# Up products of the last batch as seven products of quarters

## The chip, the cores and the metric

The kernel runs on one core of one Trainium2 chip. The metric is the device time of one execution in microseconds (us). TensorE (PE in the profile) multiplies matrices and writes into PSUM, its accumulators, which come in banks of 512 fp32 columns; VectorE (DVE), ScalarE (ACT) and GpSimd (POOL) work on elements; SyncE (SP) issues most of the DMAs. A matmul on TensorE takes a weight tile of 128x128, loaded ahead by an instruction of its own (PEld), and streams a number of columns past it. Each engine takes its instructions in the order in which the kernel's code emits them.

## What is computed

Windowed attention with a few global keys (4 batches, 8 heads, 768 positions, head dimension 64), and then a mixer on its output x (4 x 768 x 512):

```python
h = xt @ U @ V                       # xt = x.transpose(0, 2, 1); rank 32
u = x + h.transpose(0, 2, 1)
ch = np.maximum(u @ w_ch1, 0.0) @ w_ch2      # 512 -> 2048 -> 512
return (u + ch).astype(np.float32)
```

The product `u @ w_ch1` is called *up* here, the product with `w_ch2` *down*.

## The kernel before

**Attention** runs over 16 pairs of heads, `i = 0..15`, four per batch, in one loop whose body is a list of steps written out by hand: scores (`st_S`), the exponential on ScalarE (`st_E`), the product with v (`st_V`), the low-rank part (`st_M1`, `st_MT`, `st_M3`), and a DMA transpose (`st_X`, L522) that writes one 128-row slice of `uT`, the transposed u in fp16. The instructions keep the order in which the code emits them (`manual_schedule`).

**The mixer** of batch b starts when its four slices of `uT` are on their way. `queue_ff(b)` calls `queue_group` for each of three groups of 256 tokens and puts closures into two queues, `ups_q` and `downs_q`. A call `fill(n)` between the steps of attention takes n units; `unit` takes ups and downs in turn, keeps a down product back until all ups of its group are out, and lets the ups run at most one group ahead. After the loop, `while ups_q or downs_q: fill(1)` empties both. After each unit `fill` also takes one job (two when more than four are waiting) out of `jobs`, or out of `slow` when `jobs` has none that is due; these are sums that VectorE makes. `need(...)` emits a sum that is still queued when its reader comes. Each sum goes through `queue_sum` (its instruction is at L571).

**An up unit** (`mk_up`) is eight matmuls of 256 columns (L653) into one bank, with the tag `th` (three banks): two 128-wide slices of hidden columns by four slices of 128 of the 512 inputs. A ReLU on ScalarE (L658) moves the bank's 512 columns to `htr` in fp16. Eight units make a group.

**The down side** of batches 1 to 3 is already made of seven products of quarters (`mk_product`, matmuls at L707, x1, y1, x2, y2, x3, y3, x4 in this order), each eight matmuls of 256 columns. Two banks (`cx`, `cy`, tag `cps`) collect them, and after each product VectorE adds the bank to `x_sb` (L712). Their left factors are quarters of `htr` (two halves of the hidden columns by two halves of the tokens) and the sums `s1` to `s4` of these; their right ones are quarters of `w_ch2` and the sums `t1` to `t4`, made once. `queue_sums` queues `s1` to `s4` for each half of the hidden columns' slices as the ReLUs come out.

**Buffers that the change touches.** `sp` (fp32 scores, one buffer) is last read by the exponential of pair 15; `ep` (exponentials, two buffers) by `st_V` of pairs 14 and 15; `qst`, `kst` and `vst` are the staging of q, k and v. In PSUM, `sc` (two banks) and `ob` (one) belong to attention.

Of the kernel before, what the change touches and what calls it, by code (L numbers as in the profile page):

```python
# [11 lines left out]
FP32 = mybir.dt.float32  # L12
FP16 = mybir.dt.float16
# [7 lines left out]
def kernel(  # L21
# [13 lines left out]
    nc = tc.nc  # L35
# [30 lines left out]
    HJ = NJC // 2  # L66
    HD = DM // 2
    WG = tuple((b, g) for b in range(1, B) for g in range(NFG))

    cst = ctx.enter_context(tc.tile_pool(name="cst", bufs=1))  # L70
    wbig = ctx.enter_context(tc.tile_pool(name="wbig", bufs=1))
# [8 lines left out]
    def ps_sc():  # L80

        return psum.tile([P, 2, 512], FP32, name="sc", tag="sc", bufs=1)

    def ps_ob():
        return psum.tile([P, 512], FP32, name="ob", tag="ob", bufs=1)
# [4 lines left out]
    def ps_th(name, dtype=FP32, cols=512):  # L90
        return psum.tile([P, cols], dtype, name=name, tag="th", bufs=3)
# [428 lines left out]
    def st_X(i):  # L520
        b, dc = i // NP, i % NP
        nc.sync.dma_start_transpose(  # L522
            uTs[b][:, dc].rearrange("d (n p) -> d n p", n=NSB),
            x16s[i].rearrange("p n d -> p (n d)"),
        )
# [42 lines left out]
    def queue_sum(name, part, out_, a, b_, op, wait=0):  # L568

        def go():  # L570
            nc.vector.tensor_tensor(out_, a, b_, op)  # L571
            have.add((name, part))
        (slow if name[0] == "t" else jobs).append((count[0] + wait, go, name))

    def need(*names):

        for queue, kind in ((jobs, tuple), (slow, str)):
            while not all(n in have for n in names if isinstance(n[0], kind)):
                queue.popleft()[1]()
# [19 lines left out]
    def weight(w, j):  # L599
        return tw[w][:, j] if w != "t3" else tw[w][j // 2][:, j % 2]  # L600

    first_ups = []

    def queue_ff(b):
        for g in range(NFG):
            queue_group(b, g)
        if b == 0:
            for c in range(4):
                for made in first_ups:
                    ups_q.extend(made[2 * c:2 * c + 2])  # L610

    def queue_group(b, g):
# [60 lines left out]
        def mk_down(t, part):  # L673
            n = 2 * g + t

            def go():
                if (b, g, t, part) == (0, 0, 1, 0):
                    queue_weight_sums()
                if part == 0:
                    cell[t] = ps_cps("cps")  # L680
                    if b == 0:
                        nc.tensor.matmul(
                            cell[t], v16w[:, n * P:(n + 1) * P], tmp16,
                            start=True, stop=False,
                        )
                cps, htr = cell[t], cell["htr"]
                for jc in range(4 * part, 4 * part + 4):
                    nc.tensor.matmul(  # L688
                        cps, htr[:, jc, t * P:(t + 1) * P], w2_16[:, jc],
                        start=(b > 0 and jc == 0), stop=(jc == NJC - 1),  # L690
                    )
                if part == NJC // 4 - 1:
                    nc.vector.tensor_tensor(x_sb[:, n], cps, x_sb[:, n], ALU.add)
                    store(n)
            return go
# [18 lines left out]
                    store(*what)  # L714
            return go

        if b:
            for at in range(NJC // 2):
                ups_q.append((mk_up(at), (b, g)))
        else:  # L720
            first_ups.append([(mk_up(at), (b, g)) for at in range(NJC // 2)])
        if split:
            x1 = mk_product("cx", lo, "a11", "b11", (n0, lo), first=True)
            x2 = mk_product("cx", lo, "s2", "t2", (n0, hi_))
            x3 = mk_product("cx", lo, "s3", "t3", (n1, hi_), done=[(n1, hi_)] if last else None)
            x4 = mk_product("cx", lo, "a22", "t4", (n1, lo), done=[(n1, lo)] if last else [(n1,)])
            y1 = mk_product("cy", lo, "a12", "b21", (n0, lo), first=True)
            y2 = mk_product("cy", hi_, "s1", "t1", (n1, hi_))
            y3 = mk_product("cy", hi_, "s4", "b22", (n0, hi_), done=[(n0,)])
            for made in (x1, y1, x2, y2, x3, y3, x4):  # L730
                downs_q.append((made, (b, g)))
        else:
            order = [(t, part) for t in range(2) for part in range(NJC // 4)]
            if (b, g) == (0, 0):
                order.sort(key=lambda u: max(1, u[1]))
            for u in order:
                downs_q.append((mk_down(*u), (b, g)))

    ahead, held, kept = [0], [True], deque()

# [2 lines left out]
    def fill(n, quiet=False):  # L743
        for _ in range(n):
            unit()
            count[0] += 1
            pops = owed[0] + (2 if len(jobs) > 4 else 1)
            owed[0] = 1 if quiet else 0
            if jobs and jobs[0][2][0] == "s1" and not (ups_q or drained[0]):
                pops = 2  # L750
            for _ in range(0 if quiet else pops):
                for queue in (jobs, slow):
                    if queue and queue[0][0] < count[0]:
                        queue.popleft()[1]()
                        break
# [79 lines left out]
    for i in range(NP, NPAIR + 2):  # L835
        b, hp = divmod(i, NP)
        live = i < NPAIR
        units = iter(
            (0, 1, 1, 2, 1, 1, 1, 1, 1) if i == NP
            else (0, 1, 1, 1, 1, 1, 1, 1, 1) if i + 1 < NPE  # L840
            else (1, 1, 1, 2, 1, 1, 1, 1, 1)
        )
        held[0] = i < NP + 3
        if hp == 0 and live and b + 1 < B:
            new_batch(b + 1)
        if live and i > NP:
            st_S(i, 0)
        if NPE <= i + 1 < NPAIR:
            turn(i + 1)
        if i + 1 < NPAIR and i != NP + 2:  # L850
            load_v(i + 1)
        if i + 2 < NPE:
            load_qk(i + 2)
        fill(next(units))
        if NPE + 2 <= i + 2 < NPAIR:
            cast_one(i + 2, 1, nc.scalar)
        if NP < i <= NPAIR:
            st_V(i - 1, 0)
        if i == NP:
            load_w1(2)  # L860
        if i + 1 < NPE:
            st_T(i + 1)
        if i == NP:
            load_w1(3)
        fill(next(units))
        joined = live and i >= NPE - 1
        if joined:
            mid = st_S12(i)
        elif live:
            st_S(i, 1)  # L870
        fill(next(units), quiet=i > NP + 1 and (i - 2) % NP == NP - 1)
        if NP < i <= NPAIR:
            st_V(i - 1, 1)
        if joined:
            s_dve(i, mid)
        if live:
            cast_v(i)
            st_A(i)
        if NPE + 2 <= i + 2 < NPAIR:
            cast_one(i + 2, 0, nc.scalar)  # L880
        if NPE <= i + 3 < NPAIR and i != NP + 2:
            load_qk(i + 3)
        if i > NP + 1 and (i - 2) % NP == NP - 1:
            queue_ff((i - 2) // NP)
            ahead[0] = 1
        if i == NPAIR + 1:
            break
        fill(next(units))
        if live and not joined:
            st_S(i, 2)  # L890
        fill(next(units))
        if i > NP:
            st_M1(i - 1)
        else:
            for xo, o, rb in later:
                nc.vector.tensor_tensor(xo, o, rb, ALU.mult)
        if i == NP + 1:
            load_w2(0)
            load_w2(1)
        if i + 2 < NPE:  # L900
            cast_qk(i + 2, nc.gpsimd)
        if i == NP + 1:
            load_w2(2)
            load_w2(3)
        if live:
            st_E(i, 0)
            if i < NPE:
                st_P(i)
        fill(next(units), quiet=i > NP)
        if i > NPE:  # L910
            for _ in range(min(2, len(kept))):
                kept.popleft()()
        if i > NP:
            st_MT(i - 1)
        if NPE <= i + 1 < NPAIR:
            st_K(i + 1)
        fill(next(units))
        if i > NP:
            st_M3(i - 1)
        if live:  # L920
            st_E(i, 1)
        if i > NP + 1:
            st_X(i - 1)
        fill(next(units))
        if i == NP + 1:
            load_v(i + 2)
            load_qk(i + 4)
            st_X(i - 1)
        if i == NPE:
            for _ in range(2):  # L930
                kept.popleft()()
        if NPE <= i + 2 < NPE + 2:
            cast_qk(i + 2, nc.gpsimd)
        held[0] = i < NP + 2
        fill(next(units))
# [39 lines left out]
```

## Time and profile before

| | |
|---|---|
| median of 3 runs (lowest to highest) | 228.5 us (228.26 to 228.91) |
| the profiled execution: its own time, its span | 227.39 us, 225.6 us |
| busy share of the span: PE, PEld | 97%, 76% |
| busy share of the span: DVE, ACT, POOL | 69%, 56%, 33% |
| granted TensorE clock | 1.00 |
| up matmuls of 256 columns (L653), all batches | 756, 273 ns each |
| up ReLUs (L658) | 96, 600 ns each |

The span runs from the first instruction of the program to the last; the time of the execution is 1.8 us longer. Durations are those of single instructions; matmuls overlap, so the time from one start to the next is shorter than the duration. The text calls engines by name; lines of the profile use the short forms. "L653" is line 653 of the kernel before. In the rows of groups the columns are line, engine, operation, output<-inputs, shapes and count, then busy time and the mean of one in ns, then idle time before them and what ended it.

### The profile page before, as it was taken

To read this page: it belongs to the slowest core of one execution; us is meant where nothing else is said; L and a number is where in the kernel's file an instruction comes from. 1 tells how busy PE (TensorE), PEld (TensorE's weight loads), DVE (VectorE), ACT (ScalarE), POOL (GpSimd) and SP (SyncE) were. 2 spreads that over 40 slices of the span, in tenths; PEclk is the share of its full clock that TensorE was granted. 3 is DMA by queue.
4 is the path that set the end of the run, shared out by engine and by line. 5 is a ranking of instruction groups with operands and counts; after the bars stand their busy time and mean duration, and the time that the engine had idled before them with its cause. 6 is when DMAs were issued, how large, how long until landed. Compare 5 with 4: busy or idle time off the path is not lost.

```text
span 225.6 us, 5876 instructions
## 1 busy us (share of the span) xinstructions
PE 218.0 (97%) x2420; PEld 171.4 (76%) x2420; DVE 156.1 (69%) x320; ACT 126.2 (56%) x197; POOL 73.8 (33%) x124
## 2 busy tenths in 40 slices
PE   7989999999999999999999999999999999999993
PEld 2456678788754547888888888888998888888882
DVE  3798665749488988598989698898575534435552
ACT  6777867685806254967584947473733433333320
POOL 6498828297547412231313132313111000000000
PEclk9999999999999999999999999999999999999999
DMA  6999999969998999998989994960622102020112
GB/s 193 316 287 257 283 219 238 324 120 172 195 169 177 195 230 232 209 255 200 195 224 220 252 229 116 140 170 12 102 59 77 53 1 96 0 93 3 46 49 94
DMA packets 86563, 36.68 MB, mean 163 GB/s; under 512 B 74152, under 2 KB 83592, under 8 KB 86536
## 3 DMA queue, kind: packets, MB, share of 16 engines
q1 hardware_dynamic: 81480, 32.01, 60.6%
q0 software_dynamic: 5056, 4.29, 12.7%
q8 instruction: 19, 0.31, 0.6%
q14 instruction: 8, 0.07, 0.1%
HBM read 27.46 MB, written 6.29 MB: 150 GB/s over the span
## 4 chain that ended last, share of the span: by engine, by line
PE 85%; DVE 8%; ACT 2%; DMA 2%; issue 0%; SPq 0%
PE hps L653 35%; PE cx L707 13%; PE cy L707 10%; PE cps L688 9%; PE sc L367 3%; PE tp L254 3%; PE ob L448 2%; PE ob L444 2%; PE sc L533 2%; DMA kst<-in_k_dram 2%; PE sc L374 2%; ACT ep L431 1%; DVE x_sb L467 1%; DVE sp L413 1%; DVE x_sb L712 1%; DVE kA L290 1%
## 5 line engine op out<-in xcount | busy, mean ns | idle before, releaser
L653 PE MATMUL hps<-uT,w 128*128 128x256 f16 x756 | 95.0, 273 | 0.0
L658 ACT ACTIVATE htr<-hps 128x512 f16<-128x512 f32 x96 | 56.6, 600 | 55.7 <-PE hps L653 55.7
L653 PEld LDWEIGHTS <-w 128*128 128x128 f16 x756 | 71.2, 98 | 9.1
L413 DVE SCALAR_TENSOR_TENSOR sp<-sc,relcat 128x1024 f32<-128x1024 f32 (+1 forms) x27 | 32.1, 1189 | 8.5 <-PE sc L374 4.1
L431 ACT ACTIVATE ep<-sp 128x1408 f16<-128x1408 f32 x24 | 33.2, 1384 | 0.0
L470 POOL CAST x<-x_sb 128x384 f16<-128x384 f32 x27 | 14.2, 527 | 48.3 <-DVE x_sb L467 44.8
L707 PEld LDWEIGHTS <-htr 128*128 128x128 f16 x288 | 27.2, 98 | 3.1
L712 DVE TENSOR_TENSOR x_sb<-cx,x_sb 128x256 f32<-128x256 f32 x36 | 15.2, 421 | 19.0 <-PE cx L707 18.3
L688 PE MATMUL cps<-w,htr 128*128 128x512 f16 x96 | 23.9, 379 | 0.0
L707 PEld LDWEIGHTS <-s 128*128 128x128 f16 x216 | 20.4, 98 | 2.7
L541 POOL CAST x<-x_sb 128x768 f16<-128x768 f32 x12 | 10.2, 851 | 31.2 <-DVE x_sb L538 31.2
L712 DVE TENSOR_TENSOR x_sb<-cy,x_sb 128x256 f32<-128x256 f32 x27 | 11.4, 422 | 12.6 <-PE cy L707 12.4
L467 DVE TENSOR_TENSOR x_sb<-ob,rcp 128x384 f32<-128x384 f32 x30 | 16.7, 558 | 1.1
L367 PEld LDWEIGHTS <-kT 64*128 64x128 f16 x192 | 8.6, 93 | 11.5 <-issue 10.1
L448 PE MATMUL ob<-v,ep 128*128 128x65 f16 x192 | 16.4, 194 | 0.0
L367 PE MATMUL sc<-qT,kT 64*128 64x128 f16 x192 | 15.7, 220 | 0.0
L448 PEld LDWEIGHTS <-ep 128*128 128x128 f16 x192 | 13.8, 98 | 2.0 <-issue 0.3
L688 PEld LDWEIGHTS <-htr 128*128 128x128 f16 x96 | 8.4, 98 | 8.3
L444 PE MATMUL ob<-vA,ep 128*128 128x65 f16 x160 | 14.3, 194 | 0.2 <-DVE vA L317 0.2
L142 POOL CAST v<-vst 128x768 f16<-128x768 f32 x16 | 13.5, 842 | 3.0 <-DMA vst<-in_v_dram 3.0
L538 DVE TENSOR_TENSOR x_sb<-sc,x_sb 128x768 f32<-128x768 f32 x12 | 11.5, 958 | 4.0 <-PE sc L533 3.9
L374 PE MATMUL sc<-qT,kA 64*128 64x128 f16 x160 | 13.3, 217 | 0.8 <-DVE kA L290 0.6
(111 smaller groups left out, 319.2 us busy)
## 6 DMA issues: line engine op xcount, KB each, us to landing
qst<-in_q_dram SPq DMA_DIRECT2D x16, 384.0 KB, 4.0
kst<-in_k_dram SPq DMA_DIRECT2D x16, 384.0 KB, 5.7
vst<-in_v_dram SPq DMA_DIRECT2D x16, 384.0 KB, 4.0
out_dram<-x_sb SPq DMA_DIRECT2D x23, 256.0 KB, 2.0
w<-in_moe_w_ch_dram POOLq DMA_DIRECT2D x8, 512.0 KB, 8.1
vA<-v SPq DMA_DIRECT2D x8, 152.3 KB, 3.3
out_dram<-x_sb SPq DMA_DIRECT2D x2, 128.0 KB
uT<-x SPq DMA_TRANSPOSE x12, 4.4
```

The costliest lines, as they stand in the source:

```text
L367: nc.tensor.matmul(scs[hi][:, o:o + P], kT[r, kb * P:(kb + 1) * P], qT[r, kb * P:(kb + 1) * P], start=(o == 0 and not on_pe), stop=(o + P ...
L374: nc.tensor.matmul(scs[hi][:, o + P:o + 2 * P], kA[r, kb], qT[r, (kb + 1) * P:(kb + 2) * P], start=False, stop=(o + 2 * P == tot),)
L413: nc.vector.scalar_tensor_tensor(out=sps[i][:, :, c0:c0 + tot], in0=both[:, :, 0:tot], scalar=qk_scale / slope[2 * (i % NP)], in1=relfs[c0 ...
L431: nc.scalar.activation(eps[i][:, hi], sps[i][:, hi], AF.Exp, scale=slope[2 * (i % NP)])
L444: nc.tensor.matmul(ob[:, qi], ep[:, OF[qi - 1]:OF[qi - 1] + P], vA[:, qi - 1, hi], start=True, stop=False,)
L448: nc.tensor.matmul(ob[:, qi], ep[:, DG[qi]:DG[qi] + P], vt[:, qi, hi], start=(qi == 0), stop=True,)
L467: nc.vector.tensor_tensor(xo, ob[:, :, 0:D], rb, ALU.mult)
L653: nc.tensor.matmul(hps[:, k * FT:(k + 1) * FT], w1_16[:, dc, jt * P:(jt + 1) * P], uT[:, dc, ts], start=(dc == 0 and k == 0), stop=(dc == ...
L658: nc.scalar.activation(cell["htr"][:, 2 * jp:2 * jp + 2].rearrange("p j t -> p (j t)"), hps, AF.Relu)
L688: nc.tensor.matmul(cps, htr[:, jc, t * P:(t + 1) * P], w2_16[:, jc], start=(b > 0 and jc == 0), stop=(jc == NJC - 1),)
L707: nc.tensor.matmul(ps, cell[a][:, j], weight(w, j), start=(first and j == 0), stop=(done is not None and j == HJ - 1), skip_group_check=True,)
L712: nc.vector.tensor_tensor(x_sb[:, n, cs], ps, x_sb[:, n, cs], ALU.add)
```

## The change

For the last batch (`WU`), the up product of a group is written as u's transpose in quarters: A is `w_ch1` transposed in quarters (two halves of hidden columns, two halves of inputs), B is `uT` in quarters (two halves of inputs, two halves of the 256 tokens). Seven products take the place of eight. The hidden columns are handled in two parts `st` of 8 slices each (4 from each half), so a group has 14 products instead of 8 up units. A product is eight matmuls of 128 columns: four slices of hidden columns by two of inputs.

- **Weight sums**, `s1` to `s4` of quarters of `w_ch1`, for both parts: eight sums of 128x1024 fp16 on VectorE. Those of part 0 go into staging buffers (`qst`, `kst`), those of part 1 into the room that `sp` had. `queue_up_sums` puts the first four into `slow` at the end of step i = 15 and three more at the end of step i = 16; the eighth is emitted after row 4.
- **Token sums**, `t1` to `t4` of quarters of `uT`: four of 128x256 per group on VectorE, into rooms that `ep` had, emitted after the rows that `between` names.
- **Products.** In each part, products 1, 6, 7 and 4 accumulate in one bank of `th` (x), product 2 goes to the bank of `ob` (z), products 5 and 3 accumulate in one of the two banks of `sc` (y). After 2, 3 and 5 ScalarE copies the bank to SBUF (`p2`, `p3`, `p5`). After 1, 6 and 7 VectorE adds the x bank and one of these copies into a quarter of `htr`, and ScalarE applies the ReLU there in place. After 4 ScalarE applies the ReLU from the bank.
- **Rows.** The units in `ups_q` are now 22 rows (8, 7 and 7 per group), most with two products, in an order written out by hand:

```diff
+        for _, g in WU:
+            first = g == WU[0][1]
+            if first:
+                rows += [[(g, 0, 2), (g, 0, 1)], [(g, 0, 5), (g, 0, 6)], [(g, 0, 3), (g, 1, 5)]]
+            else:
+                rows[-2].insert(0, (g, 0, 5))
+                rows[-1].insert(0, (g, 0, 2))
+                rows += [[(g, 0, 1), (g, 0, 3)], [(g, 0, 6), (g, 1, 5)]]
+            rows += [[(g, 1, 2), (g, 0, 7)], [(g, 1, 1), (g, 0, 4)], [(g, 1, 3), (g, 1, 6)],
+                     [(g, 1, 7)], [(g, 1, 4)]]
+        between = {k: uw["sums"][1][x:x + 1] for k, x in ((4, 3),)}
+        for k, (_, g) in enumerate(WU):
+            for at, x in ((7 * k - 2, (0, 1)), (7 * k, (2,)), (7 * k + 1, (3,))):
+                if k == 0:
+                    at += 2
+                between.setdefault(at, []).extend(todo[g][y] for y in x)
```

The triples are group, part, product. The product itself:

```diff
+            bank, a, t = {
+                1: ("x", "a11", "b11"), 2: ("z", "a12", "b21"), 3: ("y", "s4", "b22"),
+                4: ("x", "a22", "t4"), 5: ("y", "s1", "t1"), 6: ("x", "s2", "t2"),
+                7: ("x", "s3", "t3"),
+            }[k]
...
+            for j in range(4):
+                for dc in range(2):
+                    nc.tensor.matmul(
+                        ps[:, j * P:(j + 1) * P], uw[st][a][:, dc, j * P:(j + 1) * P],
+                        turns[g][t][:, dc], start=(k in (1, 2, 5) and j == 0 and dc == 0),
+                        stop=(k in (2, 3, 4) and j == 3 and dc == 1), skip_group_check=True,
+                    )
+            early = g == WU[0][1] and st == 0
+            if k in (2, 3, 5):
...
+                nc.scalar.copy(part["p5", st] if k == 5 else part[f"p{k}"], ps)
+            if k == 1:
+                add(g, st, 0, 0, ps, part["p2"])
+            elif k == (3 if early else 6):
+                add(g, st, 0, 1, made[at, "x"], part["p3"])
+            elif k == 7:
+                add(g, st, 1, 1, ps, part["p5", st])
+            elif k == 4:
+                nc.scalar.activation(
+                    out_of(g, st, 1, 0), ps.rearrange("p (j t) -> p j t", j=4), AF.Relu
+                )
+                sums[g](st)
```

`add` is one VectorE add and one in-place ReLU:

```diff
+            nc.vector.tensor_tensor(to, x, y, ALU.add)
+            nc.scalar.activation(to, to, AF.Relu)
```

The groups of the last batch no longer put `mk_up` into `ups_q`; the down products and their sums are as before.

More of the change, by code (lines that the diff above doesn't have):

```diff
@@ L68 @@
     WG = tuple((b, g) for b in range(1, B) for g in range(NFG))
+    WU = tuple((B - 1, g) for g in range(NFG))
     cst = ctx.enter_context(tc.tile_pool(name="cst", bufs=1))
@@ L600, in weight, with up_sums @@
         return tw[w][:, j] if w != "t3" else tw[w][j // 2][:, j % 2]
+    uw, part = {}, {}
+    def up_sums():
+        made = {0: [], 1: []}
+        room = scp.tile([P, 2 * W], FP32, name="uw", tag="sp", bufs=1)
+        later_set = room[:, 0:16 * P].bitcast(FP16).rearrange("p (x d n) -> p x d n", x=4, d=2)
+        part["p2"] = room[:, 16 * P:20 * P]
+        for st in range(2):
+            js = [slice(h * DFF // 2 + st * 4 * P, h * DFF // 2 + (st + 1) * 4 * P) for h in range(2)]
+            w = {f"a{h + 1}{d + 1}": w1_16[:, 2 * d:2 * d + 2, js[h]] for h in range(2) for d in range(2)}
+            for x in range(4):
+                if st == 0:
+                    tag = ("qst", "kst")[x % 2]
+                    w[f"s{x + 1}"] = stp.tile([P, 2, 4 * P], FP16, name="uw", tag=tag, bufs=2)
+                else:
+                    w[f"s{x + 1}"] = later_set[:, x]
+            uw[st] = w
+            for name, a, b_, op in (
+                ("s1", "a21", "a22", ALU.add), ("s2", "s1", "a11", ALU.subtract),
+                ("s4", "a12", "s2", ALU.subtract), ("s3", "a11", "a21", ALU.subtract),
+            ):
+                made[st].append((f"tw{name}", st, w[name], w[a], w[b_], op))
+        return made
@@ new lines, in queue_up_sums, with token_sums @@
+    def queue_up_sums(st):
+        if st == 0:
+            uw["sums"] = up_sums()
+        for k, x in enumerate(uw["sums"][st][0:3 if st else 4]):
+            queue_sum(*x, wait=k)
+    turns = {}
+    def token_sums(g, t):
+        uT = uTs[B - 1]
+        q_ = {f"b{d + 1}{h + 1}": uT[:, 2 * d:2 * d + 2, g * FT + h * P:g * FT + (h + 1) * P]
+              for d in range(2) for h in range(2)}
+        q_.update({f"t{x + 1}": t[:, x] for x in range(4)})
+        turns[g] = q_
+        return [(f"tu{g}{n}", 0, q_[n], q_[a], q_[b_], ALU.subtract) for n, a, b_ in (
+            ("t1", "b12", "b11"), ("t2", "b22", "t1"), ("t3", "b22", "b12"), ("t4", "b21", "t2")
+        )]
@@ new lines, in queue_products, with out_of, add, step @@
+    def queue_products(b, cells, sums):
+        yy = ps_sc()
+        made = {}
+        rooms = [scp.tile([P, W], FP32, name="tu", tag="ep") for _ in range(2)]
+        places = [rooms[g // 2][:, g % 2 * 4 * P:(g % 2 + 1) * 4 * P] for g in range(NFG)]
+        part["p3"] = rooms[1][:, 4 * P:8 * P]
+        todo = {
+            g: token_sums(g, places[g].bitcast(FP16).rearrange("p (x d n) -> p x d n", x=4, d=2))
+            for _, g in WU
+        }
+        def out_of(g, st, h, t):
+            return cells[g]["htr"][:, h * HJ + 4 * st:h * HJ + 4 * st + 4, t * P:(t + 1) * P]
+        def add(g, st, h, t, x, y):
+            to = out_of(g, st, h, t)
+            x, y = (z.rearrange("p (j t) -> p j t", j=4) for z in (x, y))
+            nc.vector.tensor_tensor(to, x, y, ALU.add)
+            nc.scalar.activation(to, to, AF.Relu)
+        def step(g, st, k):
+            at = (g, st)
+            if "htr" not in cells[g]:
+                cells[g]["htr"] = ffp.tile([P, NJC, FT], FP16, name="htr", tag="htr", bufs=3)
+            if k == 1:
+                made[at, "x"] = ps_th("hps")
+            elif k == 2:
+                made[at, "z"] = ps_ob()
+            elif k == 5:
+                made[at, "y"] = yy[:, st]
+            bank, a, t = {
[3 more added lines that the diff above has]
+            }[k]
+            if a[0] == "s":
+                need((f"tw{a}", st))
+            if t[0] == "t":
+                need((f"tu{g}{t}", 0))
+            ps = made[at, bank]
+            for j in range(4):
[7 more added lines that the diff above has]
+            if k in (2, 3, 5):
+                if k == 5:
+                    part["p5", st] = stp.tile([P, 4 * P], FP32, name="p5", tag="vst", bufs=2)
+                nc.scalar.copy(part["p5", st] if k == 5 else part[f"p{k}"], ps)
+            if k == 1:
+                add(g, st, 0, 0, ps, part["p2"])
[8 more added lines that the diff above has]
+                sums[g](st)
+        rows = []
+        for _, g in WU:
+            first = g == WU[0][1]
+            if first:
+                rows += [[(g, 0, 2), (g, 0, 1)], [(g, 0, 5), (g, 0, 6)], [(g, 0, 3), (g, 1, 5)]]
+            else:
+                rows[-2].insert(0, (g, 0, 5))
[9 more added lines that the diff above has]
+                between.setdefault(at, []).extend(todo[g][y] for y in x)
+        def mk_row(n):
+            def go():
+                for s_ in rows[n]:
+                    step(*s_)
+                for x in between.pop(n, ()):
+                    nc.vector.tensor_tensor(*x[2:])
+                    have.add(x[:2])
+            return go
+        for n, row in enumerate(rows):
+            ups_q.append((mk_row(n), (b, row[-1][0])))
@@ L602 @@
     first_ups = []
     def queue_ff(b):
+        cells, sums = {}, {}
         for g in range(NFG):
-            queue_group(b, g)
+            cells[g], sums[g] = queue_group(b, g)
+        if (b, 0) in WU:
+            queue_products(b, cells, sums)
         if b == 0:
@@ L715, in mk_product @@
             return go
-        if b:
+        if (b, g) in WU:
+            pass
+        elif b:
             for at in range(NJC // 2):
@@ L737, in queue_group @@
                 downs_q.append((mk_down(*u), (b, g)))
+        return cell, queue_sums
     ahead, held, kept = [0], [True], deque()
@@ L923 @@
             st_X(i - 1)
+        if NPAIR - 1 <= i:
+            queue_up_sums(i - NPAIR + 1)
         fill(next(units))
```

## The prediction

> **What bounds the kernel now.** I read the page first, then the chain of waits over the last 50 us, then the windows of that stretch, then its groups of instructions by shape.
>
> ```profile
> PE 218.0 (97%) x2420; PEld 171.4 (76%) x2420; DVE 156.1 (69%) x320; ACT 126.2 (56%) x197; POOL 73.8 (33%) x124
> ...
> PE   7989999999999999999999999999999999999993
> ...
> DVE  3798665749488988598989698898575534435552
> ```
>
> TensorE (PE) is busy 97% of the span, VectorE (DVE) is nearly full while attention lasts and half idle in the last quarter. The chain of waits, start and duration first, shows who sets the pace there:
>
> ```profile
> 176.38 0.87 PE cx L707 x8
> 177.25 0.87 PE hps L653 x8
> 178.13 0.87 PE cy L707 x8
> ...
> 187.74 1.75 PE hps L653 x16
> ```
>
> Blocks of eight matmuls follow each other with no gap: 0.873 us for eight of 256 columns, 109.2 ns each. Up blocks (hps, L653) alternate with down products (cx, cy). By the timeline the last batch's 24 up blocks run from 177.1 to 215.5; after them come seven down products, and the last add and its store. So this stretch is bound by TensorE alone. The windows (PE, PEld, DVE, ACT, POOL, then clock, DMA share, GB/s) and the groups show what room its helpers have:
>
> ```profile
> 177.10:215.50 38.40, 38.40 (x354) 34.42 (x352) 17.45 (x41) 13.77 (x23) 0.00 (x0) 1.00 0.10 37
> ```
>
> ```profile
> L653 PE MATMUL hps<-uT,w 128*128 128x256 f16 x192 | 24.4, 273 | 0.0
> ...
> L712 DVE TENSOR_TENSOR x_sb<-cx,x_sb 128x256 f32<-128x256 f32 x12 | 5.1, 424 | 12.6 <-PE cx L707 12.4
> ```
>
> VectorE is busy 17.45 of 38.4 us, ScalarE (ACT) 13.77, at the full granted clock (1.00).
>
> **The change, part by part.**
>
> *The matmuls.* Removed: 192 of 256 columns, 192 x 109.2 ns = 20.97 us. Added: 3 groups x 14 products x 8 = 336 of 128 columns. The trace has that shape, with a fresh 128x128 weight load for each:
>
> ```profile
> 168.90 0.50 PE L533 MATMUL sc<-tmp,v16w 128*128 128x128 f16 x6
> 169.23 1.04 PE L653 MATMUL hps<-uT,w 128*128 128x256 f16 x8
> ```
>
> Six start between 168.90 and 169.23: 55 to 56 ns each. I take 55.8, so a product of eight is 0.446 us and 336 x 55.8 ns = 18.75 us. TensorE saves 2.22 us, all of it on the path.
>
> Could the weight loads not keep up? Attention's 65-column matmuls, also with a 128x128 load each, start 30 ns apart (eleven from 154.04 to 154.38), so a load is no bound at 56 ns here. The Trainium skill, page "TensorE: Matmul & The Clock Gate", section "Back-to-back issue gap", has a sustained load-and-matmul rate of about 81 ns at 128 columns; by it 336 take 27.2 us, and the sum would be 6.2 us of loss instead of 2.2 us of gain. The runs of six and eleven here disagree, but none is as long as the new rows.
>
> *What now stands between the products.* Before, a block needed only a ReLU afterwards. Now products 1, 6, 7 and 4 of one half of the hidden columns pile up in one PSUM bank, and each may start only when VectorE's add has read the bank. Prices, by rows of this trace: a copy out of PSUM on ScalarE (128x512) 0.60 (L658: 600 ns, L391: 594); an add of PSUM and SBUF (128x512) 0.681 (L693); a token difference (128x256 f16) 0.284, an estimate from L571's 0.417 at 512 and 0.683 at 1024 elements; a ReLU in place 0.61, an estimate from L340 (600 elements, 0.689) and L198 (768, 0.832). From the end of one engine's instruction to the start of the next's the trace shows 0.037 us for TensorE to VectorE or ScalarE, 0.033 for ScalarE to VectorE, 0.055 for VectorE to TensorE; two independent VectorE instructions overlap by 0.08, two of ScalarE by 0.11. A last matmul of 128 columns ends 0.219 after its start, so a product's result is there 7 x 0.0558 + 0.219 = 0.61 us after the product starts.
>
> With these I walked the queues from 176.2 on, engine by engine, in the order in which the code emits them. TensorE then waits in these places:
>
> 1. *Opening of each group* (three times). The row before product 5 has two products: first the one whose result is copied (2 for group 0, 3 of the group before for the others), then the one that is added. Copy from 0.647 to 1.247, add from 1.28 to 1.96, then t1, queued behind that add, from 1.88 to 2.165; product 5 may start at 2.22. TensorE is there after two products and one down product: 0.893 + 0.873 = 1.766. It waits 0.455; three times, 1.37 us.
> 2. *Product 4 of group 0's second half.* Rows 6 and 7 follow with no down product between them (eight rows against seven downs). After product 7: 0.61 + 0.037 + 0.681 + 0.055 = 1.383, against two products, 0.893; with 0.09 of queue on VectorE 0.58 us.
> 3. *End of the last group*, where rows hold one product, as no group follows. Product 7 waits for the same copy and add as in 1, without t1: 2.016 against 0.893 + 0.873 = 1.766, 0.25 us. Product 4: 1.383 against 0.446 + 0.873 = 1.319, 0.06, and 0.24 more since a half-sum (L571) and a down product's add (L712) are ahead on VectorE: 0.30 us.
>
> Sum: 1.37 + 0.58 + 0.25 + 0.30 = 2.50 us of waits against 2.22 us saved: +0.28 us. Elsewhere the cover holds: between two products on one bank lie at least a product's own time, a down product and a row mate, 0.446 + 0.873 + 0.446 = 1.765 us, against 1.383, or 1.57 where the add also waits for the copy of the product just before. If VectorE's queue eats those 0.2 to 0.4 us, each of these places waits too.
>
> *Off the path.* VectorE gains 18 adds (12.3 us), 12 token differences (3.4) and one weight sum (0.74): 17.45 + 16.4 = 33.9 of 38.4 us, 88%. ScalarE goes from 24 ReLUs to 42 copies and ReLUs of 0.6: 14.4 to 25.3 us, 66%; each ReLU stands behind its add and holds the next copy, which the walk includes. Seven weight sums (L571, 1024 elements, 0.74 each) run between 160 and 172, where VectorE is busy 9.18 of 17.1 us. There they can delay the normalisation of the last pair (L453, L467) by up to 0.7 us; the matmuls of the next head, the ReLU blocks and the M steps leave about that much, so I price it at 0, and at 0.3 if the cover is short. The last transpose into uT is issued at 171.4 and lands 3.6 us later in the median; the first product comes at 177.1 and so has 2 us. No DMA is added or moved.
>
> *Bounds.* If every hand-over to TensorE takes 0.1 us more, the walk grows by about 0.6; if add and ReLU each take 0.07 more, by 0.7 to 0.8. If t1 is ready in time everywhere, 0.95 us of wait goes.
>
> **The numbers.** The profiled execution took 227.39 us (span 225.6), 1.1 below the median of the runs, 228.5. On its own clock it becomes 227.39 + 0.28 = 227.7; against the median 228.8. About 0.3%, 0.7 us, is what a measurement can tell from no change.
>
> **Rivals.**
>
> - *VectorE becomes the bound (slower).* Place: the six half-groups. VectorE works in order, and an add waiting for a copy on ScalarE holds the token differences, half-sums and x_sb adds behind it. At 88% load, 4.5 us of the 38.4 are left. For it: each of 18 adds needs 0.25 us of such idle time to use that up. Against it: the walk, which has these blocks, keeps the interior products unblocked. It decides once an add and what is ahead of it take about 0.1 us longer than I put it: then the interior products 6, 7 and 4 wait too. With 0.1 at the hand-over and 0.1 in the add, the loss is 0.28 + 0.6 + 0.8 = 1.7 us: 230.2. Chance 0.35.
> - *The waits are mostly covered (faster).* If t1 and t2 come in time and the last group's adds find VectorE free, 1.37 + 0.3 us of waits vanish, and 0.83 stays against 2.22: -1.4 us, 227.1. For it: VectorE is idle for long pieces before L712 (12.6 us by the group's row). Against it: copy, add and t1 are in a fixed order with measured durations. Chance 0.22.
> - *Weight loads set the pace after all (much slower).* The load's record is 98 ns (PEld L653: 18.7 us for 191). Were each load served alone, 336 x 98 = 32.9 us against 20.97: +12 us, 240. Against it: 56 and 30 ns between starts. Chance 0.03. By the rate of the Trainium skill's page cited above it would be an estimated 234.7.
>
> **How the chances follow.** The forecast, waits and saving nearly equal, within 0.3%: 0.40. Faster 0.22. Slower 0.35 + 0.03 = 0.38. The range reaches from near the covered case, 227.3, to just past VectorE's case, 230.4; it leaves out the load-bound case, a full saving with no waits (226.3) and a far worse queue.
>
> **What would show it.** TensorE: matmuls of L653's successor at 55 to 56 ns from start to start, products of 0.45 us in the chain; at 80 ns or more the matmul price is wrong. Idle time of TensorE, now zero in this stretch, should be about 2.5 us, ended by VectorE, in pieces of 0.45 before product 5 of each group, 0.6 before product 4 of group 0, and 0.25 to 0.3 in the last group's lone products. VectorE near 34 us and ScalarE near 25 in the stretch. If the waits lie at products 6 and 7 of every group, the second case holds; if the first product starts later than 177.1, the weight sums cost what I put at nothing.

## The result and the profile after

The changed kernel takes 230.24 us (median of 6 runs, 229.7 to 230.7), the kernel before 228.38 us in the runs beside it; the ratio is 1.0103, 95% interval 1.0079 to 1.0126. By that ratio it is slower by about 2.3 us (1.8 to 2.9), where I had forecast 228.8 and no measurable difference. The medians themselves lie 1.9 us apart; the ratio is made from fast executions alone, since now and then one falls into a slower state (here 230.42 us of the kernel before), and the spreads given below leave such executions out as well. The profiled execution took 230.7 us, its span is 228.9.

Page of the changed kernel, the lines that answer to those of before:

```profile
PE 218.2 (95%) x2562; PEld 171.9 (75%) x2564; DVE 174.6 (76%) x358; ACT 136.1 (59%) x215; POOL 73.6 (32%) x124
...
PE   7889999999999999999999999999999898999993
...
DVE  3688665749498988598798797798996776877772
```

VectorE stays busy to the end, as it should with its new adds, but TensorE's row has eights in the last quarter, where before there were only nines. Who makes TensorE wait is in the changed kernel's waits of TensorE (us in total, times, longest). In the changed kernel L690 is a product of quarters, L699 ScalarE's copy of a bank, L736 a token sum (L737 in e7), L665 an add and L666 the ReLU behind it, L707 the ReLU of product 4 (in the kernel before that number was a down product), L572 a sum of the queue; L851 is a down product (L862 in e4 and e5) and L856 its add:

```profile
PE sc L690 <- ACT tu L699: 1.4, 3, 0.7
...
PE sc L690 <- DVE tu L736: 1.0, 3, 0.3
PE hps L690 <- DVE htr L665: 0.4, 1, 0.4
```

The second line is what I had called the opening of each group, the third the wait ahead of product 4 of group 0's second half. (The profile counts idle time from the modelled end of the matmul before, which is 0.16 us less than from start to start; the last group's two waits are too short for its list.) The first line, the largest, is in no step of the prediction. The timeline of the changed kernel shows one of its three cases:

```profile
182.10 0.61 PE L690 MATMUL sc<-uT,uw 128*128 128x128 f16 x8
182.40 0.41 DVE L856 TENSOR_TENSOR x_sb<-cx,x_sb 128x256 f32<-128x256 f32 x1
182.75 0.59 ACT L699 COPY tu<-sc 128x512 f32<-128x512 f32 x1 [1.13 <-PE sc L690]
183.37 0.69 DVE L665 TENSOR_TENSOR htr<-hps,tu 128x512 f16<-128x512 f32 x1 [0.55 <-ACT tu L699]
183.38 0.61 PE L690 MATMUL sc<-tu,uw 128*128 128x128 f16 x8 [0.67 <-ACT tu L699]
```

At 182.10 product 3 of the first half writes the first bank of `sc`. ScalarE copies that bank from 182.75 to 183.34. Product 5 of the second half, which writes the second bank, follows product 3 in the same row; it starts only at 183.38, 0.04 us after the copy. It reads nothing that the copy writes. Both rows name `tu`, but the copy fills `p3` and the product reads t1; in groups 0 and 1 these lie in two different buffers of that name, in group 2 in two parts of one buffer.

To compare kernels without the run-to-run differences of the first 170 us (the profiled executions reach the same point of attention up to 2.3 us apart), I take from each trace two stretches: A, from the first product with v of the last pair but one to the last M3 step (151.26 to 168.90 before), and B, from the first down product of the group ahead of the last batch (176.22 before) to the end. Wait is the sum over B of what lies between two starts of matmuls beyond 109.2 or 55.8 ns.

| kernel | A, us | B, us | waits in B, us |
|---|---|---|---|
| before | 17.64 | 49.37 | 0 |
| changed | 17.81 | 51.72 | 4.54 |
| tiles apart (e1) | 17.82 | 49.81 | 2.66 |
| t1, t2 first (e2) | 17.82 | 50.19 | 3.04 |
| product 5 a row later (e3) | 17.82 | 49.83 | 2.65 |
| all, first order (e4) | 17.82 | 48.51 | 1.35 |
| all, second order (e5) | 17.82 | 48.06 | 0.89 |
| extra VectorE work (e7) | 17.82 | 51.62 | 4.48 |
| weight sums alone (e6) | 17.82 | 49.36 | 0 |

In every row with the new products B is 49.37 - 2.22 + waits, to within 0.05. So the matmul price holds, and the waits are the rest of the story: 51.72 - 49.37 = 2.35 us in B and 0.17 in A make 2.5 us, within what the runs show (2.3, 1.8 to 2.9).

### The profile page after: what moved, and what is told of

Same layout as the page of the kernel before. It is cut to its first block, busy times and chain, and to the rows that moved or that the text cites. A ratio compares the mean times of both kernels' runs of the same rounds, so it can differ in the third digit from the quotient of the medians.

```text
span 228.9 us, 6249 instructions
## 1 busy us (share of the span) xinstructions
PE 218.2 (95%) x2562; PEld 171.9 (75%) x2564; DVE 174.6 (76%) x358; ACT 136.1 (59%) x215; POOL 73.6 (32%) x124
## 4 chain that ended last, share of the span: by engine, by line
PE 72%; DVE 12%; ACT 7%; DMA 3%; issue 2%; SPq 1%; POOL 1%; ACTq 0%
PE hps L797 25%; PE cx L851 11%; PE cps L832 9%; PE cy L851 7%; DVE htr L665 4%; DMA vst<-in_v_dram 3%; PE sc L368 3%; PE ob L449 2%; PE sc L534 2%; PE tp L255 2%; PE ob L445 2%; PE hps L690 2%; ACT htr L666 2%; ACT tu L699 2%; PE sc L690 2%
## 5 line engine op out<-in xcount | busy, mean ns | idle before, releaser
L797 PE MATMUL hps<-uT,w 128*128 128x256 f16 x564 | 70.6, 273 | 0.0
L802 ACT ACTIVATE htr<-hps 128x512 f16<-128x512 f32 x72 | 42.2, 601 | 34.1 <-PE hps L797 34.1
L797 PEld LDWEIGHTS <-w 128*128 128x128 f16 x564 | 52.4, 98 | 7.0
L851 PEld LDWEIGHTS <-htr 128*128 128x128 f16 x288 | 26.7, 98 | 2.9
L832 PE MATMUL cps<-w,htr 128*128 128x512 f16 x96 | 23.9, 379 | 0.0
L856 DVE TENSOR_TENSOR x_sb<-cx,x_sb 128x256 f32<-128x256 f32 x36 | 15.1, 420 | 11.2 <-PE cx L851 10.6
L851 PEld LDWEIGHTS <-s 128*128 128x128 f16 x216 | 20.0, 98 | 2.5
L666 ACT ACTIVATE htr<-htr 128x512 f16<-128x512 f16 x18 | 11.3, 630 | 14.8 <-DVE htr L665 14.8
L856 DVE TENSOR_TENSOR x_sb<-cy,x_sb 128x256 f32<-128x256 f32 x27 | 11.3, 419 | 4.9 <-PE cy L851 4.7
L690 PEld LDWEIGHTS <-uw 128*128 128x128 f16 x192 | 11.7, 98 | 4.0 <-issue 2.6
L832 PEld LDWEIGHTS <-htr 128*128 128x128 f16 x96 | 8.4, 97 | 8.3
```

The costliest lines, as they stand in the source:

```text
L690: nc.tensor.matmul(ps[:, j * P:(j + 1) * P], uw[st][a][:, dc, j * P:(j + 1) * P], turns[g][t][:, dc], start=(k in (1, 2, 5) and j == 0 and ...
L797: nc.tensor.matmul(hps[:, k * FT:(k + 1) * FT], w1_16[:, dc, jt * P:(jt + 1) * P], uT[:, dc, ts], start=(dc == 0 and k == 0), stop=(dc == ...
L802: nc.scalar.activation(cell["htr"][:, 2 * jp:2 * jp + 2].rearrange("p j t -> p (j t)"), hps, AF.Relu)
L832: nc.tensor.matmul(cps, htr[:, jc, t * P:(t + 1) * P], w2_16[:, jc], start=(b > 0 and jc == 0), stop=(jc == NJC - 1),)
L851: nc.tensor.matmul(ps, cell[a][:, j], weight(w, j), start=(first and j == 0), stop=(done is not None and j == HJ - 1), skip_group_check=True,)
L856: nc.vector.tensor_tensor(x_sb[:, n, cs], ps, x_sb[:, n, cs], ALU.add)
```

## Experiments

Theory 1: TensorE waits in a few fixed places, for chains of copy, add and token sum, and three of them come from the two banks of one PSUM tile being treated as one thing. Theory 2, the prediction's slower rival: VectorE is full, and the waits are its queue.

**e1, y's banks in tiles of their own.**

```diff
-                made[at, "z"] = ps_ob()
+                made[at, "z"] = ps_th("zps")
...
-                made[at, "y"] = yy[:, st]
+                made[at, "y"] = ps_ob() if st else yy[:, 0]
```

> The edit: products 5 and 3 of the second half of hidden columns get a PSUM tile of their own (the bank with tag ob) instead of the second bank of the two-bank tile sc; product 2 moves from ob to a buffer of th. Same instructions, same order, same load on VectorE and ScalarE. Theory 1 (the two banks are one tile to the waits: product 5 of the second half waits for ScalarE's copy of product 3 of the first half): the three waits of 0.84, 0.53 and 0.53 us vanish, 1.9 us, from 230.2 to about 228.3, and TensorE's other waits stay (3 x 0.5, 0.57, 0.30, 0.28: 2.6 us). Theory 2 (VectorE is the bound, as in the prediction's slower rival): its load is the same, so the waits go elsewhere, and the time stays above 229.8.

Measured: 228.76 us, ratio to the kernel before 1.0041 (1.0015 to 1.0066). The timeline of e1 at the place shown above:

```profile
181.79 0.61 PE L690 MATMUL sc<-uT,uw 128*128 128x128 f16 x8
182.24 0.61 PE L690 MATMUL ob<-tu,uw 128*128 128x128 f16 x8
182.69 1.04 PE L851 MATMUL cy<-t,s 128*128 128x256 f16 x8
```

Product 5 (now into `ob`) starts 0.45 us after product 3, with no wait. In e1's waits of TensorE, ScalarE's copy is gone and the others stand as they were:

```profile
PE sc L690 <- DVE tu L736: 1.0, 3, 0.3
...
PE hps L690 <- DVE htr L665: 0.4, 1, 0.4
```

B is 1.91 us shorter, with the same instructions on VectorE and ScalarE. Theory 2 asked for 229.8 or more, and is wrong as the explanation of these 1.9 us. Nor can it have been the buffer `tu`: e1 leaves it as it was, and in group 2, where copy and product use two parts of one buffer, product 5 now starts while the copy still runs:

```profile
207.59 0.57 ACT L699 COPY tu<-sc 128x512 f32<-128x512 f32 x1
207.68 0.61 PE L690 MATMUL ob<-tu,uw 128*128 128x128 f16 x8
```

**e2, t1 and t2 ahead of the row's products.** In `mk_row`, the `t1` and `t2` that `between` holds for a row are emitted before the row's `step` calls and not after them.

> The edit: t1 and t2 of each group are emitted ahead of the products of their row instead of behind them, so that they do not stand behind that row's add on VectorE. Theory 1 (waits by a fixed order of copy, add and difference, VectorE itself not full): the three opening waits of 0.50 us vanish, 1.5 us, from 230.2 to about 228.7; the waits of the two-bank tile stay at 1.9. Theory 2 (VectorE is the bound): the adds come 0.5 us later and products 6 and 7 wait instead; 230 or more.

Measured: 228.68 us, ratio 1.0034 (1.0002 to 1.0066); B is 1.53 us shorter than in the changed kernel. The three opening waits are gone, and the adds, which now start later, hold up nothing else. What is left in e2's waits are the other two lines:

```profile
PE sc L690 <- ACT tu L699: 1.4, 3, 0.7
...
PE hps L690 <- DVE htr L665: 0.4, 1, 0.4
```

**e3, product 5 of the second half one row later.** Tiles and load as in the changed kernel.

```diff
-                rows += [[(g, 0, 2), (g, 0, 1)], [(g, 0, 5), (g, 0, 6)], [(g, 0, 3), (g, 1, 5)]]
+                rows += [[(g, 0, 2), (g, 0, 1)], [(g, 0, 5), (g, 0, 6)], [(g, 0, 3)]]
...
-                rows += [[(g, 0, 1), (g, 0, 3)], [(g, 0, 6), (g, 1, 5)]]
-            rows += [[(g, 1, 2), (g, 0, 7)], [(g, 1, 1), (g, 0, 4)], [(g, 1, 3), (g, 1, 6)],
+                rows += [[(g, 0, 1), (g, 0, 3)], [(g, 0, 6)]]
+            rows += [[(g, 1, 5), (g, 1, 2), (g, 0, 7)], [(g, 1, 1), (g, 0, 4)], [(g, 1, 3), (g, 1, 6)],
```

> The edit: product 5 of the second half moves one row later in each group, ahead of product 2 of that half, so that a down product lies between product 3 of the first half and it; the tiles stay as they are. Theory 1: the wait for the copy (result 0.61 us after the product starts, then a copy of 0.6) is covered by 0.446 + 0.873 us, so the same 1.9 us go as with tiles of their own: about 228.3. If what costs is two banks of one tile in use at once, rather than the wait, the time stays near 230.

Measured: 228.68 us, ratio 1.0029 (1.0003 to 1.0055); B 49.83, as in e1. The two banks are still used in turn, and the time goes as soon as one more down product lies between product 3 and product 5. So it was the wait that cost, and either cure takes it away.

**e4, all of it, with a first order for the places left.** Tiles as in e1, `t1` and `t2` as in e2, and two rows changed:

```diff
+                if g == WU[1][1]:
+                    rows[-1].insert(1, (g, 0, 1))
+                    rows += [[(g, 0, 3)], [(g, 0, 6), (g, 1, 5)]]
...
+            mid = [[(g, 1, 1), (g, 0, 4)], [(g, 1, 3), (g, 1, 6)]]
+            if g == WU[-1][1]:
+                mid = [[(g, 1, 1), (g, 1, 3)], [(g, 0, 4), (g, 1, 6)]]
```

> The edit: tiles apart as in the first run, t1 and t2 ahead as in the second, and two more changes of order: product 1 of group 1's first half goes ahead of product 4 of group 0's second half (a third product of cover), and in the last group product 3 of the second half goes one row earlier, product 4 of the first half one later. Theory 1: 1.9 + 1.5 + 0.5 + 0.2 = 4.1 us of the waits vanish, 0.4 stay: 230.2 - 4.1 = 226.1, about 2.3 us faster than the kernel before, ratio 0.990. Theory 2: VectorE, busy 30.8 of 40.9 us in this stretch now, has to do the same in 37 us, 83%, and holds TensorE somewhere: 228 or more.

Measured: 228.01 us, ratio 0.9997 (0.9966 to 1.0027); B is 48.51, 3.2 us shorter than in the changed kernel and not 4.1. The expectation missed a new wait of 0.81 us, inside a down product. The timeline of e4:

```profile
193.18 0.60 PE L862 MATMUL cy<-w,htr 128*128 128x256 f16 x4
193.26 0.63 ACT L666 ACTIVATE htr<-htr 128x512 f16<-128x512 f16 x1 [0.76 <-DVE htr L665]
...
193.80 0.58 ACT L707 ACTIVATE htr<-hps 128x512 f16<-128x512 f32 x1
...
194.43 0.61 PE L862 MATMUL cy<-w,htr 128*128 128x256 f16 x4 [0.65 <-ACT htr L707]
```

The product that I had put ahead of product 4 brings a ReLU on ScalarE that waits for its add. Product 4's own ReLU stands behind it, and y1 needs that one for its last four matmuls. The runs, from 226.15 to 229.51, do not resolve the 0.7 us that A and B together give.

**e5, another order.** As e4, but group 1 gives product 3, which ends in a copy, in place of product 1; and in the last group product 4 of the first half goes ahead of product 7 of the second.

```diff
+                if g == WU[1][1]:
+                    rows[-1].insert(1, (g, 0, 3))
+                    rows += [[(g, 0, 1)], [(g, 1, 5), (g, 0, 6)]]
...
+            end = [[(g, 1, 1), (g, 0, 4)], [(g, 1, 3), (g, 1, 6)], [(g, 1, 7)]]
+            if g == WU[-1][1]:
+                end = [[(g, 1, 1), (g, 1, 3)], [(g, 1, 6)], [(g, 0, 4), (g, 1, 7)]]
```

> The edit: tiles apart and t1, t2 ahead as before, and another order at the two places left. In group 1 product 3 of the first half (not product 1) goes ahead of product 4 of group 0's second half, so that ScalarE gets a copy there and no ReLU that stands behind an add; the row after it has product 1 alone. In the last group product 3 of the second half goes two rows ahead of product 7, and product 4 of the first half stands in front of product 7. Theory 1: of the 1.35 us that TensorE still waited in the run before, the 0.81 us in the down product y1 go, and 0.2 to 0.3 of the last group's 0.43; the stretch from the last group's first down product to the end, 48.5 us in that run and 49.4 in the kernel before, becomes 47.4 to 47.7. Time: 228.4 - 1.7 to 2.0 + 0.2 for the weight sums, 226.6 to 226.9. Theory 2 (VectorE is the bound): 48.5 or more, the waits only move.

Measured: 226.76 us, ratio 0.9947 (0.9920 to 0.9974): faster than both kernels. B is 48.06, less gain than the 47.4 to 47.7 expected. That the time still lies in the expected 226.6 to 226.9 is luck in part: the kernel before took 227.97 beside these runs, not the 228.4 that the expectation counted from. The 0.81 us are gone; of the 0.89 left, 0.58 are a new wait in the last down products: product 4 comes later, so the half-sums of its part come later, and x2 waits for the last of them. e5's waits of TensorE have one line in this stretch:

```profile
PE cx L862 <- DVE s L572: 0.4, 1, 0.4
```

Its windows show how full VectorE may be while TensorE hardly waits (columns as before: PE, PEld, DVE, ACT, POOL):

```profile
176.60:215.00 38.40, 38.40 (x516) 36.15 (x514) 31.84 (x74) 23.29 (x42) 0.00 (x0) 1.00 0.11 42
```

31.84 of 38.4 us, 83%, and TensorE waits 0.31 us in the rows.

**e7, more VectorE work.** On top of e1, each `t3` and `t4` is made three times.

> The edit: the run with y's banks in tiles of their own, and each t3 and t4 made three times, the same values into the same place: 12 VectorE instructions more of 0.28 us, 3.4 us of VectorE time, no new reader. Theory 1 (TensorE waits for a few fixed chains, VectorE has room between them): at most 0.6 us on the stretch of 49.8 us. Theory 2 (VectorE is the bound): about 2.4 us more (12 x 0.20 us of issue time), 231.

Measured: 230.66 us, ratio 1.0107 (1.0055 to 1.0159); B is 51.62, 1.81 us longer than e1's. That misses theory 1's bound of 0.6 by 1.2 us and lies nearer to theory 2's 2.4, but the experiment does not separate them as I had meant: product 7 or 4 reads the last of the three writes, so part of the extra work stands in front of its own reader.

```profile
PE hps L690 <- DVE htr L665: 0.8, 3, 0.4
PE hps L690 <- DVE tu L737: 0.8, 2, 0.5
```

The second line, two new waits (0.64 and 0.47 us from start to start), is that; the first has two waits more than e1's (0.35 each), at adds in the other groups that the extra sums delayed. Three sums in a row take 0.93 us there, one 0.28; of the 0.65 us more, 0.35 reach TensorE, so VectorE has about 0.3 us to spare at these rows. That it is not full rests on e1, e3 and e5, not on e7.

**e6, the weight sums alone**, with the up products of before.

> One part alone: the kernel before with seven of the eight weight sums queued and made, read by nobody, and the up products as they were. The prediction gave them 0, at most 0.3. By the changed kernel's trace, 0.17 us between the last two pairs' products with v and the last M3 step: 17.64 us in the kernel before, 17.82 here, and nothing behind it (the last stretch 49.4 us as before).

One run, 228.27 us. In its trace A is 17.82 us against 17.64, B 49.36 against 49.37. The seven sums cost 0.18 us in attention's last steps and nothing after.

## Why the prediction was wrong

The working holds nearly line by line, and one line is missing from it. By its own steps:

| step | forecast, us | in the changed kernel, us |
|---|---|---|
| 336 matmuls for 192 | -2.22 | -2.19 (B less waits) |
| opening of each group | 3 x 0.455 | 0.50, 0.50, 0.50 |
| product 4 of group 0's second half | 0.58 | 0.57 |
| last group, products 7 and 4 | 0.25, 0.30 | 0.30, 0.28 |
| product 5 of the second half | 0 | 0.84, 0.53, 0.53 |
| weight sums | 0, at most 0.3 | 0.17 |
| sum | +0.28 | +2.5 |

**The step that failed** is "Elsewhere the cover holds". I examined there the products that follow each other on one bank (1, 6, 7, 4), and gave the two y banks no line, taking them to be independent because they are different banks. They are halves of one tile, `yy`, and a write to one half waited for the read of the other. In group 0 product 5 of the second half stands directly behind product 3 of the first, and the wait, 0.84 us, lies bare. In the other groups a down product and product 6 lie between them, but there the copy itself comes late: it stands on ScalarE behind the ReLU of product 1, which waits for VectorE's add. Group 1 in the changed kernel:

```profile
194.19 0.61 PE L690 MATMUL sc<-uT,uw 128*128 128x128 f16 x8
...
195.34 0.63 ACT L666 ACTIVATE htr<-htr 128x512 f16<-128x512 f16 x1 [1.33 <-DVE htr L665]
...
195.87 0.57 ACT L699 COPY tu<-sc 128x512 f32<-128x512 f32 x1
...
196.49 0.61 PE L690 MATMUL sc<-tu,uw 128*128 128x128 f16 x8 [0.37 <-ACT tu L699]
```

So the shared tile makes these two waits, and the add and the order on ScalarE their length, 0.53 us each; together the three places cost 1.90 us. Without these waits the sum would be 2.35 - 1.90 + 0.17 = 0.6 us, and e1 and e3 measured about that: 0.4% and 0.3% slower than before, 0.9 and 0.7 us, with intervals that begin at 0.15% and 0.03%.

**The slower rival** gave 230.2, by chance near the measured time, for a reason that the runs do not bear out: e1 and e3 take 1.9 us away with VectorE's work unchanged, and e5 runs with VectorE at 83% and 0.31 us of waits in the rows. The time also lies inside the range that I gave, but only because the range's upper end, 230.4, stood for this rival. Its warning has a core: e7 shows little room at some rows.

**The faster rival** did not come as the change stood, for the reason given against it: copy, add and t1 are emitted in that order. Emitting t1 and t2 ahead (e2) brings what it promised for the openings: 1.5 us, where the rival's sum had 1.37 and the bounds only 0.95.

**The weight loads** do not set the pace. Row after row, two products start 0.44 to 0.45 us apart:

```profile
178.08 0.61 PE L690 MATMUL ob<-uT,w 128*128 128x128 f16 x8
178.52 0.61 PE L690 MATMUL hps<-uT,w 128*128 128x128 f16 x8
178.97 0.49 PE L851 MATMUL cy<-w,htr 128*128 128x256 f16 x3
```

Sixteen matmuls take 0.89 us, 55.6 ns each, a fresh weight load with each. The rate of about 81 ns that the Trainium skill gives (page "TensorE: Matmul & The Clock Gate", section "Back-to-back issue gap") does not hold for these rows, which are faster; the measurement decides.

**VectorE and ScalarE.** I had put VectorE at 33.9 us and ScalarE at 25.3 over the products. In the windows of the changed kernel from 178.1 to 219.6 they are busy 31.9 and 23.9: the instructions overlap, which the sum of durations counts twice. The single durations were right (add 0.687 for 0.681, copies 0.58 for 0.60, ReLU in place 0.63 for 0.61, token sums 0.28).

**What stays open.** That a wait joins the two banks is shown by the traces and by both cures. Not every tile is treated as one thing: the two parts of one SBUF buffer in group 2 are not joined, as e1 shows. Why the two banks of `sc` are, and whether other PSUM tiles would be, was not tried.

## What to carry to other kernels

When a change puts an accumulation in the place of independent blocks, list for each PSUM tile (not for each bank) who last read any part of it, and put a price on every next write; a walk of the queues is as good as its list of waits, and here durations from neighbouring rows priced each listed wait to 0.05 us. Seven products for eight would save an eighth of the 20.97 us of the up blocks, 2.6 us; here it is 2.2, as two matmuls of 128 columns take 111.6 ns and one of 256 takes 109.2. Each bare hand-over of copy and add eats 0.3 to 0.8 of it. So the order is the change: a copy that others wait for goes a row ahead, sums that do not depend on the row go before its add, and an instruction that waits must not stand in front of another one's only input (the 0.81 us of e4).

## What I had not expected of the hardware

With the waits gone, five products of 128 columns in a row (40 matmuls, each with its weight load) run with only about 0.1 us of idle time among them, in e5 from 187.20 to 189.53. And the executions of one kernel spread more than most of the differences studied here (e4 from 226.15 to 229.51), while stretch A came out alike to 0.01 us in all eight kernels whose instructions are alike there (17.81 to 17.82): for effects under 1% the stretch of a trace said more than the median.
